# Attention feeding a weighted expert layer on one core: another order of evacuations, sums and first products

## The chip, the cores and the metric

The kernel runs on one core of one Trainium2 chip. The metric is the device time of one launch in microseconds (us). A profile is one execution, recorded by the hardware profiler. Engines are written as in the profile: PE is the matrix engine (PEld its weight loads), DVE the vector engine, ACT the scalar engine, POOL the GpSimd engine, SP the engine that only issues transfers. Each engine works through its own list of instructions in order; semaphores hold one back until another engine or a transfer has delivered.

## The reference, cut to what matters

First a block-sorted attention, for 4 batches of 8 heads with 768 tokens of 64 numbers. A learned 8x8 matrix per head is normalised five times over rows and columns (Sinkhorn); it then mixes the 8 blocks of keys and of values, and each block of 96 queries attends to its own mixed block. After that, four experts with two layers each, weighted per token:

```
P = sort_net;  5 times: P = exp(P - max); P /= row sums; P /= column sums
k_sorted = P @ blocks of k;  v_sorted = P @ blocks of v
attn = softmax(q_block @ k_sorted_block^T / 8) @ v_sorted_block     # 96 x 96 per block
x = attn as (3072 tokens, 512)
p = domain_probs / its row sum
out = sum over e of p[:, e] * (relu(x @ w1[e]) @ w2[e])             # 512 -> 1024 -> 512
```

## The kernel before, in words

The 3072 tokens are 12 chunks of 256: chunk (b, c) is the c-th third of batch b, and g = 3b + c. The program is a single list of calls; the order of the calls is the order of instructions on each engine. While the expert layer works on batch b, the attention of batch b + 1 is done in small stages between its products. `PLANS[b]` says in which slot each stage is issued: an entry (c, n, stage, batch, pair) means slot n of chunk (b, c). In the first layer of a chunk (`chunk_first`, L770) slot 2e + g' follows half g' of expert e: 16 matmuls (L780), the evacuation with ReLU and token weight on DVE (L786), and, for some halves, sums of hidden blocks on DVE (`h_sums`, L744). The stages that matter here, all for a pair of heads:

- `st_k`, `st_v` (L388, L357): block mixing of keys and values on PE. ACT copies the result out; `st_v` for an odd pair then issues six transfers on the SP queue that lay the values out as `vs` (L375).
- `st_s` (L409): scores, into two PSUM tiles; ACT takes the exponentials (L421).
- `st_a` (L438): attention times values, again two PSUM tiles; DVE takes reciprocals and products (L430, L431) out of each tile. It needs `vs`.
- `st_x` (L457), `st_q` (L380): transposing transfers on SP; `st_n`, `st_lk`, `st_lv`: loads issued from POOL.

All stage tiles come from one PSUM pool, `psA`, with two buffers: a stage that asks for a tile waits until the reader of the tile before the last has finished. The first-layer tiles have a pool of their own, `psM`, with two buffers as well.

From batch 1's last chunk on (g = 5, called lead; then the pairs of chunks g = 6/7, 8/9, 10/11) both layers of an expert use a seven-product form (Strassen's scheme) on quarter blocks. In the first layer one unit of work `seven(g, n)` has the products p1 to p7, which use two alternating banks X and two banks Z, and four banks Q:

- p1: Z = a11 b11, and ACT copies Z into X (L1124). p2: Z += a12 b21, and `finish` on DVE (L1110) evacuates Z into the hidden block (0,0).
- p6: X += n2 n2, ACT copies X to u2 (L1131). p7: X += s3 t3, ACT copies X to u3 (L1139), DVE adds t22 = Q + u3 (L1140).
- p4: X += a22 t4, and `finish` on DVE evacuates X into block (1,0).
- p5: Q = s1 t1. p3: Q += s4 b22, DVE adds t12 = Q + u2 (L1148).
- `22` and `12`: ReLU on ACT (L1116) of t22 and t12, then the weighting on POOL (L1117) into blocks (1,1) and (0,1).

The loop in `last_first` overlaps unit e (`now`) with the rest of unit e - 1 (`prev`): now p1, prev p7, the `12` of unit e - 2, now p5, now p2, now p6, prev `22`, prev p4, prev p3. A pair of chunks has eight units of 28 matmuls with 256 columns; lead has units 1 to 3 in this loop, with 56 matmuls of 128 columns each.

The second layer (`chunk` for g = 1 and 2 from L866, `last_second` for g from 5 on) consists of products over all experts (`times`, L764, or `product`, L1217), which need the sums of hidden blocks from DVE: `h_sums` 1 (L750) and 2 (L752), then 3 (L754) and 4 (L756). Its products run in the order b11, b21, n4, t1 (needs sums 1), t2 (sums 2), b22 for the first `early` experts (sums 4), t3 (sums 3), b22 for the other experts. For g = 1 and 2 the order is b11, b21, part of n4, t1, t2, the rest of n4, t3, b22, and the product t2 is added to the output on DVE (L884) before t3 reuses its PSUM bank.

Of the kernel before, what the change touches and what calls it, by code (L numbers as in the profile page):

```python
# [12 lines left out]
ALU = mybir.AluOpType  # L13
# [4 lines left out]
def kernel(  # L18
# [18 lines left out]
    E = moe_w1.shape[0]  # L37
# [571 lines left out]
    def st_bk(b, qd):  # L609
# [16 lines left out]
            (2, 9, st_k, 2, 0), (2, 9, st_lv, 3, 0), (2, 9, st_n, 3, 0), (2, 11, st_s, 2, 0), (2, 12, st_q, 2, 2),  # L626
        ],
        1: [
            (0, 0, st_k, 2, 1), (0, 0, st_bk, 2, 1), (0, 1, st_lk, 3, 0), (0, 1, st_n, 3, 1), (0, 2, st_a, 2, 0), (0, 2, st_q, 2, 3),
            (0, 3, st_v, 2, 2), (0, 3, st_n, 3, 2), (0, 4, st_s, 2, 1), (0, 4, st_x, 2, 0), (0, 5, st_k, 2, 2),  # L630
            (0, 5, st_n, 3, 3), (0, 6, st_v, 2, 3), (0, 6, st_lv, 3, 1), (0, 7, st_s, 2, 2), (0, 8, st_k, 2, 3),
            (0, 8, st_bv, 3, 0), (0, 9, st_bk, 3, 0), (0, 9, st_lk, 3, 1), (0, 9, st_q, 3, 0), (0, 10, st_a, 2, 1),
            (0, 11, st_s, 2, 3), (0, 12, st_a, 2, 2), (0, 12, st_x, 2, 1), (0, 12, st_q, 3, 1), (0, 13, st_v, 3, 0),
# [110 lines left out]
    def h_sums(e, which, own=False, hb=None):  # L744
        h = Hb[:, homes.get(e, e)] if hb is None else hb(e)
        blk = lambda kh, tok: h[:, ds(kh * KH, KH), ds(tok * P, P)]
        sm = [Sb[:, n, e].rearrange("p (f x) -> p f x", f=KH) for n in range(4)]
        tt = nc.vector.tensor_tensor
        if which == 1:
            tt(sm[0], blk(0, 1), blk(1, 1), ALU.add)  # L750
        elif which == 2:
            tt(sm[1], sm[0], blk(0, 0), ALU.subtract)  # L752
        elif which == 3:
            tt(blk(0, 1) if own else sm[2], blk(0, 0), blk(0, 1), ALU.subtract)  # L754
        else:
            tt(blk(1, 0) if own else sm[3], blk(1, 0), sm[1], ALU.subtract)  # L756

    def times(ps, lhs, rhs, es, first=True, done=True, between=None, at=None):

        for e in es:  # L760
            if e == at:
                between()
            for f in range(KH):
                nc.tensor.matmul(  # L764
                    ps, lhs(e, f), Ts[e][rhs][:, f, :],
                    start=(first and e == es[0] and f == 0), stop=(done and e == es[-1] and f == KH - 1),
                    skip_group_check=True,
                )
# [28 lines left out]
    def chunk(b, c, slot, done=()):  # L797
# [68 lines left out]
        if c:  # L866
            both = ob.rearrange("p (h d) -> p h d", h=2)
            times(bankA, blk(0, 0), "b11", es)
            slot()
            times(bankB, blk(1, 0), "b21", es)  # L870
            slot()
            tt(oa1, bankA, oa1, ALU.add)
            tt(oa1, bankB, oa1, ALU.add)
            h_sums(E - 1, 2)
            times(bankC, blk(1, 1), "n4", es[:1], True, False)
            times(bankQ, sm(0), "t1", es)
            tt(ob2, bankQ, ob2, ALU.add)
            slot()
            for e in es:
                h_sums(e, 3)  # L880
            for e in es:
                h_sums(e, 4)
            times(bankA, sm(1), "t2", es, False)
            tt(oa2, bankA, oa2, ALU.add)  # L884
            slot()
            next(sums0)
            times(bankC, blk(1, 1), "n4", es[1:], False)
            tt(ob1, bankC, ob1, ALU.add)
            slot()
            times(bankA, sm(2), "t3", es, False)  # L890
            tt(both, bankA.rearrange("p (o d) -> p o d", o=1).broadcast_to([P, 2, DH]), both, ALU.add)
            slot()
            store(1, ob)
            next(sums0)
            times(bankQ, sm(3), "b22", es, False)
            tt(oa2, bankQ, oa2, ALU.add)
            slot()
            store(0, oa)
            return
# [180 lines left out]
    def seven(g, n):  # L1080

        lead = g == G0
        if lead:
            e, f0, cols = n, 0, P
            pb = pbs[divmod(g, R // 2)]
            home = lambda i, j: Hb[:, e, ds(i * KH, KH), ds(j * P, P)]
            weight = lambda j: pb[:, ds(e, 1), ds(j * P, P)]
            n -= 1
            Q = last["Q"][(0, 0, 1, 3)[e]][:]
        else:  # L1090
            e, f0, cols = n // 2, n % 2 * 2, 2 * P
            home = lambda i, j: (last["H"][e] if j else Hb[:, e])[:, ds(i * KH + f0, 2), :]
            weight = lambda j: pbs[g](j, e)
            Q = last["Q"][n % 4][:]
        m = 512 // cols
        a, t = As[e], Bs[g]
        X, Z = [last[nm][n % len(last[nm])][:] for nm in ("X", "Z")]
        u2, u3, t22, t12 = [last[nm][n % len(last[nm])] for nm in ("u2", "u3", "t22", "t12")]
        tt = nc.vector.tensor_tensor

        def product(dst, lhs, rhs, first=False):
            for f in range(m):
                for k in range(2):
                    nc.tensor.matmul(  # L1104
                        dst[:, ds(f * cols, cols)], a[lhs][:, k, ds((f0 + f) * P, P)], t[rhs][:, k, :],
                        start=(first and f == 0 and k == 0), stop=(f == m - 1 and k == 1), skip_group_check=True,
                    )

        def finish(i, j, src):
            nc.vector.scalar_tensor_tensor(  # L1110
                out=home(i, j), in0=src.rearrange("p (f x) -> p f x", f=m), scalar=0.0,
                op0=ALU.max, in1=weight(j).broadcast_to([P, m, cols]), op1=ALU.mult,
            )

        def finish2(i, j, src):
            nc.scalar.activation(src, src, AF.Relu, bias=0.0, scale=1.0)  # L1116
            nc.gpsimd.tensor_tensor(  # L1117
                home(i, j), src.rearrange("p (f x) -> p f x", f=m),
                weight(j).broadcast_to([P, m, cols]), ALU.mult,
            )  # L1120

        def p1():
            product(Z, "a11", "b11", True)
            nc.scalar.copy(X, Z)  # L1124

        def p5():
            product(Q, "s1", "t1", True)

        def p6():
            product(X, "n2", "n2")  # L1130
            nc.scalar.copy(u2, X)  # L1131

        def p2():
            product(Z, "a12", "b21")
            finish(0, 0, Z)

        def p7():
            product(X, "s3", "t3")
            nc.scalar.copy(u3, X)  # L1139
            tt(t22, Q, u3, ALU.add)  # L1140

        def p4():
            product(X, "a22", "t4")
            finish(1, 0, X)

        def p3():
            product(Q, "s4", "b22")
            tt(t12, Q, u2, ALU.add)  # L1148

        return {  # L1150
            1: p1, 2: p2, 3: p3, 4: p4, 5: p5, 6: p6, 7: p7,
            22: lambda: finish2(1, 1, t22), 12: lambda: finish2(0, 1, t12),
        }

# [5 lines left out]
    def last_first(g, slot=None):  # L1160
        b, c = divmod(g, R // 2)
        lead = int(g == G0)
        if lead:
            chunk_first(b, c, [0], 0, slot)
            last_banks(0)
            last_tmp(g)
            prs = {1: seven(g, 1)}
            prs[1][1]()
            prs[1][5]()
            seven(g, 2)[5]()  # L1170
            prs[1][6]()
            prs[1][2]()
            input_sums(0, 0, True)
            input_sums(0, 1, True)
            last_banks(1)
        else:
            last["e0"][2]()
            prs = {0: last["e0"]}
        N7 = E if lead else 2 * E
        for e in range(1 + lead, N7):  # L1180
            prs[e] = seven(g, e)
        for e in range(1 + lead, N7):
            now, prev = prs[e], prs[e - 1]
            now[1]()
            prev[7]()
            if e > 1 + lead:
                prs[e - 2][12]()
            if not lead or e > 2:
                now[5]()
            now[2]()  # L1190
            now[6]()
            prev[22]()
            prev[4]()
            prev[3]()
        now[7]()
        prev[12]()
        return now

    def last_second(g, now=None, upper=False):
# [12 lines left out]
        def product(ps, lhs, rhs, first=True, es=range(E), between=None, at=E - 1, part=ds(0, DH)):  # L1212
            for e in es:
                if e == at and between:
                    between()
                for f in range(KH):
                    nc.tensor.matmul(  # L1217
                        ps, lhs(e, f), Ts[e][rhs][:, f, part],
                        start=(first and e == 0 and f == 0), stop=(e == E - 1 and f == KH - 1), skip_group_check=True,
                    )  # L1220
# [27 lines left out]
            sums(e, 2)  # L1248
        product(bankC, blk(1, 1), "n4")
        nc.scalar.copy(ob1, bankC)  # L1250
        for e in range(E):
            sums(e, 4, True)
        if lead:
            for e in range(E):
# [8 lines left out]
        if not lead:  # L1263
            for e in range(E):
                sums(e, 3, True)
        early = 1 if final else 2
        for bank, part, _ in ends:
            product(bank[:, part], blk(1, 0), "b22", False, range(early), part=part)
        if closing and not final:
# [201 lines left out]
```

The softmax here doesn't subtract the row's maximum and nothing guards it: scores larger than these inputs give would overflow.

## Time and profile before

| | before |
|---|---|
| median of 4 runs | 364.1 us (362.56 to 364.68) |
| the profiled execution, its own time | 364.41 us |
| span in its profile | 362.6 us |
| PE busy | 352.7 us, 97% of the span |
| DVE busy | 272.0 us, 75% |
| ACT busy | 172.4 us, 48% |
| POOL busy | 133.5 us, 37% |
| granted PE clock | 0.9 of full speed or more in all 40 slices |

The span runs from the first to the last profiled instruction; the 1.8 us between it and the execution's own time lie around it. Start times below are counted from the span's start. In a timeline, a row gives the start and the duration of an instruction or of a group of like ones (x16), the engine, the line and the tiles (out<-in); brackets at its end give the idle time of its engine before it and what ended that. Matmuls overlap, so the time between the starts of two groups tells more than their durations.

### The profile page before, as it was taken

Reading aid. Unit: us, or ns where it says so; the run is one execution under the profiler, and the core shown is the slowest. Engines: PE = TensorE matmul, PEld = TensorE weight load, DVE = VectorE, ACT = ScalarE, POOL = GpSimd, SP = SyncE. Lnnn points to the kernel's source line nnn. Section 1 sums busy time; section 2 is a strip of 40 time slices with the busy share of each in tenths; the row PEclk is TensorE's granted clock in tenths of the full one; section 3 lists DMA queues with packets and bytes.
Section 4 is the critical chain, followed back from the end, with each engine's and each line's share of the span. In section 5 each row is a group of like instructions: output and inputs, shape, how many; then the busy total and the mean of one; then the engine's idle time right before and its main releaser. Section 6 shows DMA issues by size and latency. Waiting matters only on the chain.

```text
span 362.6 us, 9496 instructions
## 1 busy us (share of the span) xinstructions
PE 352.7 (97%) x3949; PEld 305.3 (84%) x3949; DVE 272.0 (75%) x549; ACT 172.4 (48%) x306; POOL 133.5 (37%) x148
## 2 busy tenths in 40 slices
PE   8799999999999899999999999999999999999995
PEld 8685858888888788888889888888888888888895
DVE  5654897779698677868878977895587876677962
ACT  2664330453325255367937258830388611688210
POOL 8882010476022240000526318840068800288300
PEclk9999999999999999999999999999999999999999
DMA  8999999999999999935996310005200014100011
GB/s 110 207 207 230 214 209 198 193 181 191 196 165 132 188 137 160 158 94 73 166 206 77 108 69 0 2 2 117 107 12 2 3 57 118 61 0 2 2 72 46
DMA packets 72007, 40.52 MB, mean 112 GB/s; under 512 B 40598, under 2 KB 66716, under 8 KB 71964
## 3 DMA queue, kind: packets, MB, share of 16 engines
q0 software_dynamic: 36560, 19.93, 42.0%
q1 hardware_dynamic: 35260, 19.92, 29.2%
q8 instruction: 31, 0.51, 0.6%
q14 instruction: 12, 0.10, 0.1%
q10 hardware_dynamic: 144, 0.07, 0.1%
HBM read 42.13 MB, written 6.34 MB: 134 GB/s over the span
## 4 chain that ended last, share of the span: by engine, by line
PE 84%; DMA 7%; DVE 5%; ACT 1%; SPq 1%; POOL 1%; issue 1%; ACTq 0%; DVEq 0%
PE ps_Q L1217 17%; PE ps_h L780 16%; PE ps_X L1104 10%; PE ps_p L764 8%; PE ps_Z L1104 7%; PE ps_Q L1104 7%; PE ps_Z L1217 6%; DMA w<-in_moe_w_dram 4%; PE ps_o L704 3%; PE ps_p L815 3%; DMA vs<-arena 2%; PE ps_h L669 1%; PE ps_a L449 1%; PE ps_s L414 1%; PE ps_v L361 1%; SPq L375 1%
## 5 line engine op out<-in xcount | busy, mean ns | idle before, releaser
L780 PE MATMUL ps_h<-xT,w 128*128 128x256 f16 x576 | 67.7, 273 | 0.0
L780 PEld LDWEIGHTS <-w 128*128 128x128 f16 x576 | 55.2, 98 | 7.3
L786 DVE SCALAR_TENSOR_TENSOR Hb<-ps_h,pb 128x1024 f16<-128x1024 f32 x34 | 41.5, 1224 | 17.3 <-PE ps_h L780 17.1
L1104 PEld LDWEIGHTS <-w 128*128 128x128 f16 x480 | 43.5, 98 | 6.4 <-issue 0.3
L1117 POOL TENSOR_TENSOR arena<-tmp,pb 128x512 f16<-128x512 f32 x12 | 15.3, 1275 | 65.8 <-PE ps_Z L1104 49.9
L1217 PEld LDWEIGHTS <-Hb 128*128 128x128 f16 x320 | 31.2, 98 | 3.6
L1116 ACT ACTIVATE tmp<-tmp 128x512 f32<-128x512 f32 x46 | 29.3, 638 | 3.2 <-DVE tmp L1148 2.6
L1217 PEld LDWEIGHTS <-Sb 128*128 128x128 f16 x304 | 28.2, 98 | 3.0
L1104 PEld LDWEIGHTS <-arena 128*128 128x128 f16 x312 | 27.7, 98 | 2.9
L421 ACT ACTIVATE ET<-ps_s 96x768 f16<-96x768 f32 x24 | 18.0, 802 | 25.4 <-PE ps_s L414 25.2
L404 ACT CAST kT<-ps_k 64x384 f16<-64x384 f32 x48 | 22.7, 473 | 14.1 <-PE ps_k L395 13.1
L121 POOL DMA_DIRECT2D arena<-in_q_dram x24 | 19.9, 842 | 19.5 <-DMA q_ring<-arena 19.1
L1104 PE MATMUL ps_X<-ET,arena 128*128 128x256 f16 x168 | 25.2, 272 | 0.0
L1124 ACT COPY ps_X<-ps_Z 128x512 f32<-128x512 f32 x27 | 15.4, 570 | 19.9 <-PE ps_Z L1104 15.6
L764 PEld LDWEIGHTS <-Hb 128*128 128x128 f16 x232 | 21.9, 98 | 3.0
L1217 PE MATMUL ps_Q<-w,Hb 128*128 128x256 f16 x192 | 24.4, 273 | 0.0
L1104 PE MATMUL ps_Z<-xT,w 128*128 128x256 f16 (+1 forms) x176 | 22.5, 257 | 0.2 <-ACT ps_X L1124 0.2
L1140 DVE TENSOR_TENSOR tmp<-ps_Q,tmp 128x512 f32<-128x512 f32 x20 | 13.8, 691 | 11.3 <-ACT tmp L1139 7.6
L1110 DVE SCALAR_TENSOR_TENSOR Hb<-ps_X,pb 128x512 f16<-128x512 f32 x27 | 18.4, 682 | 1.6 <-PE ps_X L1104 1.6
L750 DVE TENSOR_TENSOR Sb<-Hb 128x512 f16<-128x512 f16 x33 | 19.5, 610 | 0.0
L1131 ACT COPY tmp<-ps_X 128x512 f32<-128x512 f32 x26 | 15.2, 586 | 9.1 <-PE ps_X L1104 8.8
L1110 DVE SCALAR_TENSOR_TENSOR Hb<-ps_Z,pb 128x512 f16<-128x512 f32 x27 | 18.4, 682 | 1.3 <-PE ps_Z L1104 1.3
(261 smaller groups left out, 743.5 us busy)
## 6 DMA issues: line engine op xcount, KB each, us to landing
w<-in_moe_w_dram POOLq DMA_DIRECT2D x7, 1024.0 KB, 28.3
pb<-p_dram SPq DMA_DIRECT2D x9, 512.0 KB, 7.1
arena<-in_k_dram POOLq DMA_DIRECT2D x8, 384.0 KB, 10.2
arena<-in_v_dram POOLq DMA_DIRECT2D x8, 384.0 KB, 8.5
vs<-arena SPq DMA_DIRECT2D x36, 66.0 KB, 6.0
arena<-in_q_dram POOLq DMA_DIRECT2D x24, 96.0 KB, 9.7
out_dram<-ob SPq DMA_DIRECT2D x9, 256.0 KB, 2.1
out_dram<-oa SPq DMA_DIRECT2D x8, 256.0 KB, 2.3
```

The source lines that it names most:

```text
L121: nc.gpsimd.dma_start(t[:, h // 2, :, h % 2, :], q[b, h].rearrange("(t p) d -> p t d", p=P))
L404: nc.scalar.copy(kT[ds(D * hh, D), r], pk[ds(D * r, D), hh].rearrange("p a (i c) -> p a i c", c=CP),)
L421: nc.scalar.activation(ETs[2 * (pr % 2) + hh][:, 0:S].rearrange("c (a x) -> c a x", a=2), pss[hh][0:BLK, :, 0:HS], AF.Exp, bias=0.0, scale ...
L750: tt(sm[0], blk(0, 1), blk(1, 1), ALU.add)
L764: nc.tensor.matmul(ps, lhs(e, f), Ts[e][rhs][:, f, :], start=(first and e == es[0] and f == 0), stop=(done and e == es[-1] and f == KH - 1 ...
L780: nc.tensor.matmul(ps[:, f, :], w1sb[e][:, kc, ds((4 * g + f) * P, P)], xT[:, kc, ds(2 * c * P, 2 * P)], start=(kc == 0), stop=(kc == NKC ...
L786: nc.vector.scalar_tensor_tensor(out=Hb[:, homes.get(e, e), ds(4 * g, 4), :], in0=ps[:], scalar=0.0, op0=ALU.max, in1=weights(e).broadcast ...
L1104: nc.tensor.matmul(dst[:, ds(f * cols, cols)], a[lhs][:, k, ds((f0 + f) * P, P)], t[rhs][:, k, :], start=(first and f == 0 and k == 0), st ...
L1110: nc.vector.scalar_tensor_tensor(out=home(i, j), in0=src.rearrange("p (f x) -> p f x", f=m), scalar=0.0, op0=ALU.max, in1=weight(j).broadc ...
L1116: nc.scalar.activation(src, src, AF.Relu, bias=0.0, scale=1.0)
L1124: nc.scalar.copy(X, Z)
L1217: nc.tensor.matmul(ps, lhs(e, f), Ts[e][rhs][:, f, part], start=(first and e == 0 and f == 0), stop=(e == E - 1 and f == KH - 1), skip_gro ...
```

## The change

It moves instructions and adds none to PE, ACT, POOL or SP; the work done is the same.

1. **Plan of batch 1.** `st_a(2,0)` goes from slot 2 to slot 3 of chunk (1,0), its `st_x` from slot 4 to 5, and `st_v(2,2)` from slot 3 to slot 5, behind `st_k(2,2)`.
2. **Chunks g = 1 and 2.** The sums 4 are issued behind the product t2 and its addition (L884), not ahead of them.
3. **Pairs.** The `finish` of Z moves behind p4 of the unit before, so that DVE evacuates X ahead of Z. PE's order stays.
4. **Lead.** In the loop for e = 2 the p5 of unit 3 is placed ahead of p2, and p3 of unit 1 moves from the end of that round into the round for e = 3, where p5 was; `12` of unit 1 follows it.
5. **`last_second`.** Outside lead, the sums 4 of experts 2 and 3 move behind the sums 3. In the last chunk `early` is 2, not 1.

```diff
         1: [
-            (0, 0, st_k, 2, 1), (0, 0, st_bk, 2, 1), (0, 1, st_lk, 3, 0), (0, 1, st_n, 3, 1), (0, 2, st_a, 2, 0), (0, 2, st_q, 2, 3),
-            (0, 3, st_v, 2, 2), (0, 3, st_n, 3, 2), (0, 4, st_s, 2, 1), (0, 4, st_x, 2, 0), (0, 5, st_k, 2, 2),
+            (0, 0, st_k, 2, 1), (0, 0, st_bk, 2, 1), (0, 1, st_lk, 3, 0), (0, 1, st_n, 3, 1), (0, 2, st_q, 2, 3), (0, 3, st_a, 2, 0),
+            (0, 3, st_n, 3, 2), (0, 4, st_s, 2, 1), (0, 5, st_x, 2, 0), (0, 5, st_k, 2, 2), (0, 5, st_v, 2, 2),
             (0, 5, st_n, 3, 3), (0, 6, st_v, 2, 3), (0, 6, st_lv, 3, 1), (0, 7, st_s, 2, 2), (0, 8, st_k, 2, 3),
...
             for e in es:
                 h_sums(e, 3)
+            times(bankA, sm(1), "t2", es, False)
+            tt(oa2, bankA, oa2, ALU.add)
             for e in es:
                 h_sums(e, 4)
-            times(bankA, sm(1), "t2", es, False)
-            tt(oa2, bankA, oa2, ALU.add)
             slot()
...
+        def p2_first():
+            product(Z, "a12", "b21")
+
+        def p2_last():
+            finish(0, 0, Z)
+
...
-            1: p1, 2: p2, 3: p3, 4: p4, 5: p5, 6: p6, 7: p7,
+            1: p1, 2: p2, 3: p3, 20: p2_first, 21: p2_last, 4: p4, 5: p5, 6: p6, 7: p7,
...
             now[1]()
             prev[7]()
-            if e > 1 + lead:
+            if lead:
+                (prs[3][5] if e == 2 else prs[1][3])()
+                now[2]()
+                now[6]()
+                prev[22]()
+                prev[4]()
+                if e > 2:
+                    prs[1][12]()
+                    prev[3]()
+                continue
+            if e > 1:
                 prs[e - 2][12]()
-            if not lead or e > 2:
-                now[5]()
-            now[2]()
+            now[5]()
+            now[20]()
             now[6]()
             prev[22]()
             prev[4]()
+            now[21]()
             prev[3]()
...
         nc.scalar.copy(ob1, bankC)
-        for e in range(E):
+        early = 2
+        for e in range(E if lead else early):
             sums(e, 4, True)
...
             for e in range(E):
                 sums(e, 3, True)
-        early = 1 if final else 2
+            for e in range(early, E):
+                sums(e, 4, True)
```

## The prediction

> **What bounds the kernel now.** I read the shares of busy time first, then PE's own waits, then the chain of work that ended last, and from it the timeline of each place that the change touches.
>
> ```profile
> PE 352.7 (97%) x3949; PEld 305.3 (84%) x3949; DVE 272.0 (75%) x549; ACT 172.4 (48%) x306; POOL 133.5 (37%) x148
> ```
>
> PE is busy in 97% of the span, and the chain gives it 84%. No edit removes a matmul, so a gain can only be a gap on PE that closes, and a loss one that opens. In steady work sixteen matmuls of 256 columns take 1.75 us from start to start (chain: "PE ps_h L780 x16"), so one is 0.109 us and four are 0.44 us; I take each gap from start times against this. Four places matter.
>
> Place one, chunk (1,0):
>
> ```profile
> 119.47 3.66 PE L780 MATMUL ps_h<-xT,w 128*128 128x256 f16 x32
> 124.83 0.65 PE L449 MATMUL ps_a<-vs,ET 96*128 96x65 f16 x16 [1.70 <-DMA vs<-arena]
> 125.27 0.20 DVE L430 RECIPROCAL rz<-ps_a 96x8 f32<-96x8 f32 x1 [0.88 <-PE ps_a L449]
> 126.35 0.69 DVE L431 TENSOR_TENSOR xsl<-ps_a,rz 96x512 f16<-96x512 f32 x1
> 127.26 1.23 DVE L786 SCALAR_TENSOR_TENSOR Hb<-ps_h,pb 128x1024 f16<-128x1024 f32 x1 [0.23 <-PE ps_h L780]
> 128.85 0.42 DVE L752 TENSOR_TENSOR Sb<-Sb,Hb 128x512 f16<-128x512 f16 x1
> 129.23 0.51 PE L414 MATMUL ps_s<-q_ring,kT 64*128 64x96 f16 x16
> ```
>
> 32 matmuls from 119.47 are over at 119.47 + 3.49 = 122.96; `st_a(2,0)` starts at 124.83, when its `vs` has landed. That is a gap of 1.87 us, the largest after the opening. While PE stands, DVE is free to empty `st_a`'s tiles at once, from 125.27 to 126.35 + 0.69 = 127.04.
>
> Place two, chunk g = 1 (and the same row in g = 2):
>
> ```profile
> 88.98 1.04 PE L764 MATMUL ps_p<-T,Hb 128*128 128x256 f16 x8
> 90.34 1.47 PE L764 MATMUL ps_p<-T,Sb 128*128 128x256 f16 x12 [0.32 <-DVE room L884]
> ```
>
> Eight matmuls from 88.98 end at 89.85; t3 starts at 90.34, 0.49 late, since L884 stood in DVE's queue behind the sums 4. In g = 2 the same pair of rows (113.16 and 114.21) gives 0.18.
>
> Place three, a round of a pair:
>
> ```profile
> 226.54 0.60 PE L1104 MATMUL ps_X<-ET,w 128*128 128x256 f16 x4
> 226.83 0.68 DVE L1110 SCALAR_TENSOR_TENSOR Hb<-ps_Z,pb 128x512 f16<-128x512 f32 x1
> 227.43 0.68 DVE L1110 SCALAR_TENSOR_TENSOR Hb<-ps_X,pb 128x512 f16<-128x512 f32 x1
> 228.03 0.68 DVE L1148 TENSOR_TENSOR tmp<-ps_Q,tmp 128x512 f32<-128x512 f32 x1
> 228.22 0.57 ACT L1124 COPY ps_X<-ps_Z 128x512 f32<-128x512 f32 x1 [0.29 <-DVE Hb L1110]
> 228.28 0.60 PE L1104 MATMUL ps_Q<-kT,arena 128*128 128x256 f16 x4
> 228.84 0.60 PE L1104 MATMUL ps_Z<-xT,w 128*128 128x256 f16 x4
> 229.40 0.69 DVE L1140 TENSOR_TENSOR room<-ps_Q,room 128x512 f32<-128x512 f32 x1 [0.69 <-ACT room L1139]
> ```
>
> p5 starts at 228.28, p2 at 228.84: 0.56 where 0.44 is due. p2 waits for the copy L1124, that waits for DVE to empty X, and DVE empties Z first.
>
> Place four, lead's second layer:
>
> ```profile
> 200.50 2.57 DVE L750 TENSOR_TENSOR Sb<-Hb 128x512 f16<-128x512 f16 x3
> 201.33 1.46 POOL L1117 TENSOR_TENSOR Hb<-tmp7x,pb 128x512 f16<-128x512 f32 x1 [0.28 <-ACT tmp7x L1116]
> 203.19 1.91 PE L1217 MATMUL ps_Q<-w,Sb 128*128 128x256 f16 x16
> 203.33 0.41 DVE L750 TENSOR_TENSOR Sb<-Hb 128x512 f16<-128x512 f16 x1
> ```
>
> The sums that PE uses from 203.19 are ready hardly before; the last one waits for POOL's last multiplication, which ends at 202.79.
>
> **The change, part by part.** *Plan.* One slot later, `st_a` stands behind the sixteen matmuls of (1, second half), which now start at 122.96 and end at 124.71; `vs` allows 124.83, so 0.12 of the 1.87 stays. But DVE's queue has changed too: the evacuation of that half and two sums now stand ahead of `st_a`'s four instructions. Today this block runs 1.95 us behind its matmuls and takes 128.85 + 0.42 - 127.26 = 2.01; so 122.96 + 1.95 + 2.01 = 126.92, and `st_a`'s tiles are empty 1.77 later (127.04 - 125.27), at 128.69. `st_s(2,1)` asks for both tiles: `st_v(2,2)`, which lay between and took one, is gone. PE is ready at 124.83 + 0.48 + 1.84 = 127.15 and starts some 0.1 after DVE, about 128.8: a wait of 1.65. Queued behind it is everything on PE. `st_v(2,2)` comes 0.33 us of PE work later, behind `st_k(2,2)`; `st_v(2,3)` then needs the tile of `st_k`, which ACT copies for 1.96 us (one L404 group, now from 131.6 to 133.5), about 0.2 more than PE gives it. The SP queue gets the next six `vs` issues 0.3 later; their reader starts 3.8 us after they land today (142.3 and 146.1), which hides it. `st_x` and the loads have no near reader. Sum: -1.87 + 0.12 + 1.65 + 0.2 = **+0.1 us**. The wait changes its name from DMA to DVE.
>
> *Chunks g = 1, 2.* L884 follows t2 at once and is over before t3 is due (88.95 + 0.42 against 89.85). The sums 4 end about 0.5 us later; their reader, b22, starts at 91.6, they end at 90.4. **-0.49 - 0.18 = -0.7 us.**
>
> *Pairs.* X is emptied first: p4 starts at 226.54, and DVE follows a p4 by 0.64 where it is free (198.37 to 199.01), so X starts at 227.18, not 227.43; L1124 can then follow Z's first product. The chain's p2 rows in this pair are 0.48, 0.48, 0.56, 0.55, 0.56 for 0.44 due: 0.43 in all, and the other two pairs read alike. The other side: Z starts at 227.78 and L1148 at 228.38, 0.35 later. L1148 is over at 229.06, before L1140 can start (229.40, less the 0.17 that the copies gain on ACT: L1124 starts 0.81 after p1 today, 0.64 then). **3 x -0.43 = -1.3 us.**
>
> *Lead.* p5 of unit 3 fills the gap ahead of p2 of unit 2 (0.38: 191.62 where 191.24 was due). Yet the next p2 waits for L1124, that for DVE's X, which goes by DVE's queue (input sums until 192.29, then three evacuations), unchanged. With as much PE work ahead of it, that p2 starts at 194.82 as today: the gap moves. What does change is POOL: `12` of unit 1, at 195.88 today, goes behind `22` of unit 2, whose ReLU ends about 197.0. Five multiplications of 1.3 follow without a pause and end near 203.8, not 202.79. The fourth L750 then ends about 1.1 late. Today it ends at 203.74 and PE needs it at 203.19 + 1.31 = 204.50: 0.76 of cover, so PE waits **+0.3 us**. The bounds are 0 (DVE keeps its pace) and 1.1 (all of it reaches PE).
>
> Three L750 took 2.57 us here, against 0.415 for the median one: something beside POOL slows them. The Trainium skill, "SBUF — State Buffer", section "Who interferes with whom", says that a DVE instruction with two SBUF inputs and a GpSimd instruction that reads SBUF exclude one another for a whole instruction. That speaks against this edit, which puts one more multiplication beside these sums; taken strictly, a further sum loses a whole multiplication, and the term would be the upper bound, 1.1, not 0.3.
>
> *`last_second`.* Its sums come in the order of use now; no gap stands there today (96 matmuls in 10.48 us is 0.109 each). In the last chunk t3 waits 0.23 for ACT's copy L1262 (eight b22 matmuls of half width from 354.88 end at 355.32, t3 starts 355.55). Eight more fill that, but then DVE's three last additions follow t3 without a pause and bind: **-0.1 us.**
>
> Sum: +0.1 - 0.7 - 1.3 + 0.3 - 0.1 = -1.7 us. The profiled execution took 364.41, so 362.7; it lies 0.3 above the median of 364.1, against which the forecast is **362.4 us**.
>
> **The rivals.** *The later `st_a` pays in full.* If DVE empties its tiles before 127.15, the first term is -1.7, the time 360.6. For it: the wait on `vs` is plain in the profile. Against it: the queue above. The same pattern, `st_a` one slot ahead of `st_s`, starts today at 144.04, 0.1 behind DVE's second L431, with nothing queued ahead on DVE.
>
> *The pairs do not gain.* p2 may be held by the copy itself: L1124 follows p1 by 0.64 and takes 0.57, p2 needs it 1.31 after p1's start, so the cover is 0.1. If that is lost, the pair term is 0, the time 363.7.
>
> *Slower: L1140 slides in the pairs.* DVE now stands until p4 is through and does Z and L1148 after it. Should L1148 push L1140 by its own 0.35, then p3, due 0.06 after L1140's end (226.97 and 226.91), waits 0.29 in 7 rounds of 3 pairs, 6.1 us: 364.1 + 6.1 - 1.7 = 368.5. It decides at L1140 starting more than 1.87 us after its round's p1, since p3 falls due 6 x 0.44 = 2.62 after p1; today it is 1.99 with the gap in the round (227.41 to 229.40), and 1.81 is what I expect. Against it: 0.15 us between L1148's end and L1140's start.
>
> **How the numbers follow.** What can be told from no change is about 0.5%, 1.8 us: the bounds are 362.3 and 365.9. My forecast (0.55) lies at the edge, 0.29 beyond and 0.26 within. Full pay 0.17 (faster), no gain in the pairs 0.17 (within), sliding 0.11 (slower). Faster 0.46, same 0.43, slower 0.11. The range goes from full pay, a little rounded, 360.4, to the case where the pairs gain nothing and lead costs its upper bound, 363.7 + 0.8 = 364.5.
>
> **What would show it.** Right: `st_a` without a wait for DMA, `st_s(2,1)` idle 1.6 us for DVE L431; no wait for the bank's addition before t3; p2 rows of 0.44 in the pairs' chain, and L1124 released by PE; in lead one gap of 0.5 before unit 3's p2 and L1217 waiting for L750. Wrong: `st_s` starting before 128 us, p2 rows still at 0.55, or waits of p3 for L1140.

## The result, and the profile after

| | before | after |
|---|---|---|
| median | 364.6 us (78 runs) | 362.92 us (54 runs) |
| ratio to before, 95% interval | | 0.996 (0.9951 to 0.997) |
| the profiled execution, its own time | 364.41 us | 363.6 us |
| span in its profile | 362.6 us | 361.7 us |

The change makes the kernel 1.5 us faster (0.4%; the interval is 1.1 to 1.8 us). The forecast was 1.7 us, a time of 362.4 in a range of 360.4 to 364.5. The gain lies just inside the 0.5% that the prediction drew as its border; it gave this side 0.43 and a larger gain 0.46. The ratio leaves out the executions more than 1.5% above the fastest (3 of 54 and 4 of 78).

The page after, engine by engine: busy time, share of the span, instructions.

```profile
PE 352.2 (97%) x3949; PEld 305.9 (85%) x3949; DVE 275.2 (76%) x549; ACT 172.4 (48%) x306; POOL 133.2 (37%) x148
```

The counts are those of before. PE is 0.5 us less busy, and DVE 3 us busier with the same instructions, among them L750, whose durations sum to 26.8 us and before to 25.1 (0.9 of the difference lies in place four). The edits shift line numbers: L1148 is now L1154, L1217 is L1233, L1262 is L1279, and L884 is L882.

The view of waits, for PE, names what PE now stands for (in total, times, longest); these are its largest rows beside those of the opening (L312, L256, L563):

```profile
PE ps_s L414 <- DVE xsl L431: 1.3, 2, 0.7
PE ps_h L780 <- DMA xT<-xsl: 0.4, 1, 0.4
PE ps_a L449 <- DMA vs<-arena: 0.3, 1, 0.3
```

The 1.7 us of `st_a(2,0)` for `vs` is gone, and 1.3 us of the scores for DVE stands in its place. L884's (now L882's) wait is gone. The wait on `vs` that is left is another one, at 182 us. The timeline of place one, chunk (1,0), from `st_a` on (of the timelines here, the rows that matter):

```profile
125.08 0.65 PE L449 MATMUL ps_a<-vs,ET 96*128 96x65 f16 x16
125.28 1.22 DVE L786 SCALAR_TENSOR_TENSOR Hb<-ps_h,pb 128x1024 f16<-128x1024 f32 x1 [0.52 <-PE ps_h L780]
125.56 1.91 PE L780 MATMUL ps_h<-xT,w 128*128 128x256 f16 x16
...
126.87 0.42 DVE L752 TENSOR_TENSOR Sb<-Sb,Hb 128x512 f16<-128x512 f16 x1
127.21 0.20 DVE L430 RECIPROCAL rz<-ps_a 96x8 f32<-96x8 f32 x1
128.19 0.21 PE L414 MATMUL ps_s<-q_ring,kT 64*128 64x96 f16 x1 [0.71 <-DVE xsl L431]
128.28 0.69 DVE L431 TENSOR_TENSOR xsl<-ps_a,rz 96x512 f16<-96x512 f32 x1
129.02 0.51 PE L414 MATMUL ps_s<-q_ring,kT 64*128 64x96 f16 x15 [0.62 <-DVE xsl L431]
```

`st_a` starts without a wait. DVE has L786, L750 (126.42) and L752 to do before L430 can begin at 127.21, and the second L431 ends at 128.97. The sixteen matmuls from 125.56 are over at 127.31. The first score matmul starts when the first tile is empty, and the other fifteen, which need the second, at 129.02. One matmul of the scores takes some 0.03, so the loss is 129.02 - 127.31 - 0.03 = 1.68 us.

Place two, t3's start in chunk g = 1, and place three, a round of a pair, in the timeline after:

```profile
89.50 1.04 PE L764 MATMUL ps_p<-T,Hb 128*128 128x256 f16 x8
90.37 1.47 PE L764 MATMUL ps_p<-T,Sb 128*128 128x256 f16 x12
```

```profile
227.69 0.69 DVE L1110 SCALAR_TENSOR_TENSOR Hb<-ps_X,pb 128x512 f16<-128x512 f32 x1 [0.27 <-PE ps_X L1104]
227.92 0.60 PE L1104 MATMUL ps_Z<-xT,w 128*128 128x256 f16 x4
...
228.29 0.68 DVE L1110 SCALAR_TENSOR_TENSOR Hb<-ps_Z,pb 128x512 f16<-128x512 f32 x1
228.60 0.57 ACT L1124 COPY ps_X<-ps_Z 128x512 f32<-128x512 f32 x1 [0.16 <-PE ps_Z L1104]
228.79 0.60 PE L1104 MATMUL ps_Q<-kT,arena 128*128 128x256 f16 x4
...
229.23 0.60 PE L1104 MATMUL ps_Z<-xT,w 128*128 128x256 f16 x4
229.78 0.69 DVE L1140 TENSOR_TENSOR room<-ps_Q,room 128x512 f32<-128x512 f32 x1 [0.21 <-ACT room L1139]
```

t3 follows after 0.87, the eight matmuls' own time. In the pair p2 follows p5 by 0.44 (228.79 to 229.23), where it took 0.56. The copy L1124 is released by PE (p1, from 227.92) and no longer by DVE. L1140 is held by ACT's copy, not by L1154. Place four, the second layer of lead:

```profile
195.31 0.61 PE L1104 MATMUL ps_Z<-xT,w 128*128 128x128 f16 x8 [0.29 <-ACT ps_X L1124]
200.99 3.49 DVE L750 TENSOR_TENSOR Sb<-Hb 128x512 f16<-128x512 f16 x3
201.33 2.87 POOL L1117 TENSOR_TENSOR Hb<-tmp7x,pb 128x512 f16<-128x512 f32 x2
203.67 2.14 PE L1233 MATMUL ps_Q<-w,Sb 128*128 128x256 f16 x16
204.74 0.41 DVE L750 TENSOR_TENSOR Sb<-Hb 128x512 f16<-128x512 f16 x1
```

The gap before unit 2's p2 is gone, and one of 0.46 stands before unit 3's (195.31, where 194.85 was due). POOL has two multiplications left beside the three sums, not one; the sums take 3.49 us and not 2.57, and the fourth starts 1.07 after the product that uses it, not 0.14. That product takes 1.98 from start to the next one's start where 1.75 is due.

Matched matmul by matmul, the span's 0.89 us (after less before) divides as follows:

| stretch | us |
|---|---|
| opening: first weights arrive later (PE's L704 at 28.48, before 27.96) | +0.52 |
| chunks g = 1 and 2, L884's waits | -0.48, -0.18 |
| a wait for transposed x at 118.09 | +0.52 |
| plan, chunk (1,0) from `st_a` to 134 us | -0.06 |
| around 182 us: a wait on `vs` +0.46, one on DVE gone -0.28 | +0.18 |
| lead | +0.23 |
| three pairs | -1.33 |
| last chunk | -0.28 |

The parts that were changed sum to -2.1. The other +1.2 (opening, 118 us, 182 us) lies in stretches that the change doesn't touch. That the wait at 118 us comes from PE being earlier there, after part 2, isn't borne out: the profile of part 2 alone has no such wait. A second profile of the changed kernel (the last experiment) has neither of the two later waits, and a span of 361.0.

### The profile page after: what moved, and what is told of

It reads as the page before. It is cut to its first block, busy times and chain, and to the rows that moved or that the text cites. A ratio compares the mean times of both kernels' runs of the same rounds, so it can differ in the third digit from the quotient of the medians.

```text
span 361.7 us, 9496 instructions
## 1 busy us (share of the span) xinstructions
PE 352.2 (97%) x3949; PEld 305.9 (85%) x3949; DVE 275.2 (76%) x549; ACT 172.4 (48%) x306; POOL 133.2 (37%) x148
## 4 chain that ended last, share of the span: by engine, by line
PE 85%; DVE 7%; DMA 3%; issue 2%; ACT 2%; DVEq 0%; ACTq 0%
PE ps_Q L1233 16%; PE ps_h L780 16%; PE ps_p L764 9%; PE ps_X L1104 9%; PE ps_Q L1104 6%; PE ps_Z L1104 6%; PE ps_Z L1233 6%; PE ps_h L669 3%; PE ps_o L704 3%; PE ps_p L815 3%; DMA xT<-xsl 2%; PE ps_s L414 1%; PE ps_a L449 1%; DVE xsl L431 1%; DVE Sb L750 1%
## 5 line engine op out<-in xcount | busy, mean ns | idle before, releaser
L786 DVE SCALAR_TENSOR_TENSOR Hb<-ps_h,pb 128x1024 f16<-128x1024 f32 x34 | 41.5, 1223 | 18.7 <-PE ps_h L780 18.4
L1233 PEld LDWEIGHTS <-Hb 128*128 128x128 f16 x320 | 31.1, 98 | 3.6
L1233 PEld LDWEIGHTS <-Sb 128*128 128x128 f16 x304 | 28.0, 98 | 3.4 <-DVE Sb L750 0.3
L404 ACT CAST kT<-ps_k 64x384 f16<-64x384 f32 x48 | 22.7, 473 | 14.5 <-PE ps_k L395 13.5
L1233 PE MATMUL ps_Q<-w,Hb 128*128 128x256 f16 x192 | 24.4, 273 | 0.0
L1124 ACT COPY ps_X<-ps_Z 128x512 f32<-128x512 f32 x27 | 15.4, 570 | 18.5 <-PE ps_Z L1104 18.2
L750 DVE TENSOR_TENSOR Sb<-Hb 128x512 f16<-128x512 f16 x33 | 21.2, 660 | 0.0
L1154 DVE TENSOR_TENSOR tmp<-ps_Q,tmp 128x512 f32<-128x512 f32 x26 | 17.7, 682 | 0.8 <-PE ps_Q L1104 0.8
```

Source lines behind the costliest of these rows:

```text
L404: nc.scalar.copy(kT[ds(D * hh, D), r], pk[ds(D * r, D), hh].rearrange("p a (i c) -> p a i c", c=CP),)
L786: nc.vector.scalar_tensor_tensor(out=Hb[:, homes.get(e, e), ds(4 * g, 4), :], in0=ps[:], scalar=0.0, op0=ALU.max, in1=weights(e).broadcast ...
L1233: nc.tensor.matmul(ps, lhs(e, f), Ts[e][rhs][:, f, part], start=(first and e == 0 and f == 0), stop=(e == E - 1 and f == KH - 1), skip_gro ...
```

## The experiments

Theory: the gain is that of parts 2 and 3, with a little from 5; parts 1 and 4 move a wait and are worth about nothing. Rival: part 1 or 4 carries a part of the gain. All ratios are against the kernel before, run on the same chip beside them, with 95% intervals; 0.001 is 0.36 us. The edits are shortened.

**Part 1 alone** (plan).

```diff
-(0, 2, st_a, 2, 0) ... (0, 3, st_v, 2, 2) ... (0, 4, st_x, 2, 0)
+(0, 3, st_a, 2, 0) ... (0, 5, st_x, 2, 0) ... (0, 5, st_v, 2, 2)
```

> Only the plan's three entries are changed, everything else is the kernel before. Theory (the wait moves from DMA to DVE): ps_a starts without a wait for DMA, the next scores wait for DVE L431 for 1.3 to 1.7 us, ps_v(2,3) starts 0.2 late; sum within 0.2 us of the kernel before. Rival (the later stage pays in full): no wait of the scores, 1.7 us faster.

Measured: 1.0007 (0.999 to 1.0023), +0.25 us. The profile has the wait of the scores and none for `vs`:

```profile
124.69 0.65 PE L449 MATMUL ps_a<-vs,ET 96*128 96x65 f16 x16
127.79 0.21 PE L414 MATMUL ps_s<-q_ring,kT 64*128 64x96 f16 x1 [0.71 <-DVE xsl L431]
128.63 0.51 PE L414 MATMUL ps_s<-q_ring,kT 64*128 64x96 f16 x15 [0.62 <-DVE xsl L431]
```

The rival that the later `st_a` pays in full falls: the wait changes its name, and the time does not change measurably.

**Part 2 alone** (sums 4 behind t2).

```diff
-            for e in es: h_sums(e, 4)
             times(bankA, sm(1), "t2", es, False)
             tt(oa2, bankA, oa2, ALU.add)
+            for e in es: h_sums(e, 4)
```

> Only the order of the sums 4 and the product t2 in the chunks g = 1 and 2 is changed. Theory: t3 starts on time in both chunks, 0.49 and 0.18 us gained there; what is gained in g = 2 may be lost at once, since the first matmuls of the next chunk then wait for the transposed x (the changed kernel's profile shows 0.52 us there), so 0.3 to 0.7 us faster. Rival (the later sums 4 make b22 late): no gain.

Measured: 0.9982 (0.9965 to 0.9999), -0.65 us. L884's wait is gone in both chunks.

**Part 3 alone** (X evacuated ahead of Z in the pairs).

```diff
-            now[2]()
+            now[20]()        # p2's product alone
...
             prev[4]()
+            now[21]()        # the finish of Z
```

> Only the order of the evacuations of Z and X in the three pairs is changed. Theory: the p2 rows fall from 0.48 to 0.56 us to 0.44, 0.43 us per pair, 1.3 us faster in all; this is most of the gain of the whole change. Rival (copy L1124 itself holds p2, or L1140 slides): p2 rows unchanged or p3 rows longer, no gain or a loss.

Measured: 0.9954 (0.9935 to 0.9974), -1.7 us. Its p2 rows follow p5 by 0.44, as in the whole change. Both rivals about the pairs (no gain; L1140 sliding) fall.

**Part 4 alone** (lead's order).

```diff
             if lead:
+                (prs[3][5] if e == 2 else prs[1][3])()
                 now[2]()
...
+                if e > 2:
+                    prs[1][12]()
+                    prev[3]()
+                continue
```

> Only lead's round is re-ordered. Theory: the gap before p2 of unit 2 (0.38 us) goes and one of about 0.46 us opens before p2 of unit 3; POOL's multiplications end about 1 us later beside the sums L750, of which three take some 3.5 us instead of 2.57, and the product t1 takes 0.2 to 0.3 us more; 0.2 to 0.3 us slower than the kernel before. Rival (the filled gap is a gain): 0.4 us faster.

Measured: 1.0013 (0.9997 to 1.0029), +0.5 us. The gap stands before unit 3's p2 with the same 0.46, and the second layer is 0.23 longer.

**All parts but lead's.** The change without the edit just shown.

> The changed kernel with lead's round as before. Theory: a little faster than the changed kernel, by 0.2 to 0.5 us, so 1.7 to 2.1 us faster than the kernel before; the three L750 of lead take 2.57 us again. Rival (the filled gap helped): 0.4 us slower than the changed kernel.

Measured: 0.9941 (0.9917 to 0.9966), -2.1 us, against -1.5 for the whole. Lead's old gap (0.38 before unit 2's p2) is back and its second layer has its old length. The two intervals overlap, but together with part 4 alone they put part 4 on the side of a loss, though neither comparison is clear of zero by itself.

**Part 5 alone** (last chunk and order of the sums).

```diff
-        early = 1 if final else 2
+        early = 2            # and sums 4 of experts 2, 3 behind the sums 3
```

> Only the second layer's order of sums and the last chunk's early b22 are changed. Theory: nothing but the last chunk moves, t3 there starts without its 0.23 us wait for L1262, 0.1 to 0.2 us faster than the kernel before, not to be told from no change. Rival (the later sums 4 of two experts hold the last b22): PE rows of b22 late, up to 0.5 us slower per chunk.

Measured: 0.9987 (0.9964 to 1.001), -0.5 us, an interval that holds zero. t3 no longer waits for the copy of t2's result.

**The scores later.** If the scores' wait for DVE is the price of part 1, more PE work ahead of the scores should take it back.

```diff
-(0, 4, st_s, 2, 1), (0, 5, st_x, 2, 0), (0, 5, st_k, 2, 2), (0, 5, st_v, 2, 2), (0, 5, st_n, 3, 3),
-(0, 6, st_v, 2, 3), (0, 6, st_lv, 3, 1), (0, 7, st_s, 2, 2), (0, 8, st_k, 2, 3), (0, 8, st_bv, 3, 0),
+(0, 5, st_x, 2, 0), (0, 5, st_s, 2, 1), (0, 5, st_n, 3, 3), (0, 6, st_v, 2, 2), (0, 6, st_k, 2, 2),
+(0, 7, st_v, 2, 3), (0, 7, st_lv, 3, 1), (0, 8, st_s, 2, 2), (0, 8, st_bv, 3, 0), (0, 9, st_k, 2, 3),
```

> The changed kernel with the scores of pair (2,1) a slot later still, so that DVE has emptied both tiles of ps_a before PE asks for them; value and key stages follow one slot later each, values first. Theory (the plan's gain was lost to the tiles that DVE empties late): the scores start without a wait, ps_v(2,3) too, 1.6 to 1.8 us faster than the changed kernel, 3.1 to 3.4 us faster than before. Rival (something else is late next, a copy on ACT or the landing of the next values): the gap turns up again within the next slots and the time stays within 0.5 us of the changed kernel.

Measured: 0.9955 (0.9937 to 0.9972), -1.6 us: no gain over the change. Its PE rows:

```profile
129.31 0.52 PE L414 MATMUL ps_s<-q_ring,kT 64*128 64x96 f16 x16
130.31 1.91 PE L780 MATMUL ps_h<-xT,w 128*128 128x256 f16 x16 [0.48 <-DVE Hb L786]
142.34 1.91 PE L764 MATMUL ps_p<-T,Sb 128*128 128x256 f16 x16 [0.51 <-DVE oa L842]
```

The scores start at once. The next half of the first layer then waits for its own PSUM tile, since DVE does `st_a`'s four instructions before that evacuation, and later an addition is late behind ACT's copies. From `st_a` at 125.23 to the first product of the next chunk at 151.18 this kernel takes 25.95 us, the change from 125.08 to 151.35 takes 26.27: the scores' 1.68 and the 0.2 of `st_v(2,3)` are gone, and all but 0.3 of them comes back, a part behind DVE's queue and a part behind ACT's. That is the rival.

**Lead's input sums later.** The gap before unit 3's p2 was put down to DVE's queue, which has two input sums (L978) ahead of the evacuations.

```diff
-            input_sums(0, 0, True)
-            input_sums(0, 1, True)
             last_banks(1)
...
             now[1]()
+            if lead and e == 3:
+                input_sums(0, 0, True)
+                input_sums(0, 1, True)
             prev[7]()
```

> The changed kernel with lead's two input sums on DVE (L978, 1.28 us) moved behind unit 3's p1, where DVE stands 1.2 us. Theory (DVE's queue with those sums ahead holds X and with it p2 of unit 3): the gap of 0.46 us before that p2 goes, POOL's chain ends about as late as in the changed kernel; 0.3 to 0.5 us faster than the changed kernel. Rival (p2 is held by PE's own order or by ACT): the gap stays, no gain.

Measured: 0.9971 (0.9954 to 0.9989), -1.1 us: not faster than the change. The gap shrinks only to 0.35: with the sums gone DVE stands 1.01 us for ACT's copy L1139 before unit 1's L1140 (191.28), and X is empty at 193.17 all the same. The two sums (on DVE from 193.09) now take 2.36 us, beside a multiplication on POOL, where they took 1.28; they delay L1140, for which p3 waits:

```profile
193.21 1.68 POOL L1117 TENSOR_TENSOR Hb<-tmp,pb 128x512 f16<-128x512 f32 x1 [2.88 <-ACT tmp L1116]
195.37 0.68 DVE L1140 TENSOR_TENSOR tmp<-ps_Q,tmp 128x512 f32<-128x512 f32 x1
196.10 0.61 PE L1104 MATMUL ps_Q<-xT,w 128*128 128x128 f16 x8 [0.70 <-DVE tmp L1140]
```

The second of the two takes 1.76, from 193.69 to 195.45, for 0.68 in the change. L1140's other input, ACT's copy, was ready at 194.36. This place was wrong for them, and the run does not tell what a better one would bring.

**Parts 2, 3 and 5**, with plan and lead as before.

> Parts 2, 3 and 5 alone; plan and lead as before. Theory (the gain lies in the sums of chunks 1 and 2, in the pairs and in the last chunk, while plan and lead together are worth nothing or a small loss): -0.65 - 1.7 - 0.5 by the three kernels that have one of these parts each, -2.3 by the profile's steps (0.7, 1.3 and 0.1 to 0.3); so 2.0 to 2.8 us below before, a ratio of 0.992 to 0.9945, and 0.5 to 1.3 us below the whole change. Rival (plan and lead carry part of the gain): no lower than the whole change, a ratio of 0.996 or more.

Measured: 0.9955 (0.9936 to 0.9974), -1.6 us. The theory asked for a ratio of 0.992 to 0.9945 and its rival for 0.996 or more: the measured one lies between and decides for neither. The run shows that the gain is there without parts 1 and 4; whether those two cost anything together can't be told from these runs.

**Extra PE work ahead of `st_a`**, in the kernel before and in part 1 alone.

```diff
+                again = (b, c, e, g) == (1, 0, 0, 0)
-                for f in range(4):
+                for f in ((0, 1) if again else ()) + (0, 1, 2, 3):
```

> The kernel before, with the first eight matmuls of chunk (1,0)'s first half done twice, 0.87 us of PE work that changes no result, between the issue of vs and st_a's wait for it. Theory (vs lands at a time of its own, so the wait for it takes up what makes PE late): the wait for vs is shorter by 0.87 or gone, and the time grows by the part that the wait does not cover. With the waits seen so far before st_a (1.87, 0.97, 0.84, 0.39, 0.08) the mean cover is 0.61, so 0.26 us slower than before. Rival (the time of vs follows PE): 0.87 us slower, and the wait in the profile as long as in the kernel before.

> Part 1 alone with the same 0.87 us of extra PE work. Theory (here the scores wait for DVE, which follows PE by a fixed chain, so nothing takes up a late PE): 0.87 us slower than part 1 alone, which read +0.25, so some 1.1 us above before and 0.6 above the kernel before with the same extra work; the scores' wait for DVE stays at 1.3 us. Rival (the new wait has slack as well): within 0.3 us of the kernel before with the extra work, and the scores' wait shorter.

Measured: 1.0011 (0.9996 to 1.0027), +0.4 us, in the kernel before; 1.0036 (1.0018 to 1.0054), +1.3 us, with part 1, which is 1.06 more than part 1 alone. The two kernels' PE rows, first before's, then part 1's:

```profile
125.76 0.65 PE L449 MATMUL ps_a<-vs,ET 96*128 96x65 f16 x16 [0.94 <-DMA vs<-arena]
```

```profile
129.00 0.21 PE L414 MATMUL ps_s<-q_ring,kT 64*128 64x96 f16 x1 [0.71 <-DVE xsl L431]
129.84 0.51 PE L414 MATMUL ps_s<-q_ring,kT 64*128 64x96 f16 x15 [0.62 <-DVE xsl L431]
```

With part 1 the wait keeps its 0.71 and 0.62, and from `st_a` to the scores' second start it is 3.94 us without the extra work (124.69 to 128.63) and 3.95 with it (125.89 to 129.84): the extra 0.87 is paid in full, and the chain from PE through DVE back to PE has no slack. How much the transfer covers in the kernel before, this run doesn't tell: the interval of the +0.4 (-0.15 to +1.0) holds the theory's 0.26 and its rival's 0.87, and the wait in the profile is 1.10 by start times. The expectation worked with waits from one execution each; start times show how far these differ. From the matmul of `st_v(2,1)`, whose copy feeds `vs`, to `st_a` (one execution of each kernel with the plan of before):

| kernel | `st_v(2,1)` | PE ready | `st_a` | wait | `st_v` to `st_a` |
|---|---|---|---|---|---|
| before | 111.35 | 122.96 | 124.83 | 1.87 | 13.48 |
| part 2 alone | 111.24 | 122.67 | 123.64 | 0.97 | 12.40 |
| part 3 alone | 112.12 | 123.72 | 123.72 | 0 | 11.60 or less |
| part 4 alone | 112.29 | 124.17 | 125.00 | 0.83 | 12.71 |
| part 5 alone | 111.18 | 122.78 | 123.18 | 0.40 | 12.00 |
| parts 2, 3, 5 | 111.70 | 123.13 | 124.04 | 0.91 | 12.34 |
| before, extra work | 112.18 | 124.66 | 125.76 | 1.10 | 13.58 |

PE's own way from `st_v` to `st_a` is 11.4 to 11.9 us without the extra work. The way of the values through ACT, six issues and the transfers differs by execution. All fourteen traces have the landing of the last of the six, whether PE waited for it or not: 11.4 to 13.5 us after that matmul. The wait is the difference. For the twelve executions without extra work, and PE's own way taken as 11.6, that makes (an estimate) a wait of 0 to 1.9 in the order of before, 1.0 in the mean, and the profile of before holds the longest.

**Lead without two multiplications.** It was to show whether POOL slows the sums.

```diff
+            if g == G0 and n == 3:
+                ...              # ReLU by ACT straight into the block
+                return
```

> The whole change, but the weighting of unit 3's blocks (1,1) and (0,1) in lead is left out (ACT's ReLU writes these blocks itself), so that the last two multiplications of POOL are gone and none runs beside lead's sums. Theory (the sums are slow because of POOL's multiplications beside them): the three L750 take 0.42 each, 1.3 us or less where they start behind POOL's last one and 1.7 at most with one multiplication beside the first, not 3.49; the product t1 waits for none of them, lead's second layer is 0.23 shorter or more, and the time 0.2 to 0.5 us below the whole change. Rival (they wait for their data or for PE): three L750 still over 2.5 us.

In lead the function lowers `n` by one, so the condition never held: nothing was left out, and this is the whole change a second time. Measured: 0.9971 (0.9949 to 0.9993), which agrees with 0.996. Its three L750 take 3.50 us beside POOL's two multiplications, where the first profile has 3.49.

That POOL is the cause was not tested by taking it away. What the traces show beside that stands in the last section.

## Why the prediction was right, step by step

*Plan, +0.1.* The mechanism held: the scores lose 1.68 us for DVE where 1.65 was forecast, the second start is 129.02 where some 128.8 was forecast (`st_a` itself came 0.25 later than assumed), and `st_v(2,3)` is 0.2 late as worked out. Against this one execution the step measures -0.06, in runs +0.25 (-0.4 to +0.8). What was weak is the first term, -1.87: it came from the execution with the longest wait, and the mean by the landings above is 1.0. With that and the 1.68 and 0.2 that the scores and `st_v(2,3)` lose, plan would cost about +0.9, which the runs don't show either: part 1 alone ends its interval at +0.8, and parts 2, 3 and 5 measure -2.1 with part 1 (all parts but lead's) and -1.6 without. So that +0.1 came out near the runs is in part luck, and what takes up the rest is open.

*Chunks 1 and 2, -0.7.* In the profile -0.48 and -0.18, in runs -0.65.

*Pairs, -1.3.* In the profile -1.33, in runs -1.7 (-2.4 to -0.95). The slower rival was nearer than its 0.11 says. It decides at L1140 starting more than 1.87 after its round's p1. The change has 227.92 to 229.78, 1.86, where 1.81 was expected. What holds it is the copy L1139 on ACT, straight behind L1124, which PE releases, and not L1154; so the queue on DVE has 0.21 of room, but p3 none. The other rival was near as well: L1124 ends at 228.60 + 0.57 = 229.17, 0.06 before p2, where the cover was put at 0.1.

*Lead, +0.3.* The profile has +0.23; runs of part 4 alone +0.5 (-0.1 to +1.05). The gap moved as forecast (0.46 for "about 0.5"), POOL ends 1.4 later, and the fourth L750 starts 0.93 later against its product, of which 0.76 was covered. One reading was not right: the fourth L750 doesn't wait for POOL's last multiplication itself (over at 202.79 before, 204.20 after) but stands in DVE's queue behind the third, slowed sum (over at 203.07 and 204.48) and one addition to the output. The Trainium skill's rule ("SBUF — State Buffer", section "Who interferes with whom") fits the sums: one more of them takes 1.49 and not 0.41, which is 1.08, close to a whole multiplication. But the upper bound of 1.1 drawn from it left out the cover of the product, and the trace's row decides: +0.23.

*Last chunk, -0.1.* The mechanism is as forecast: DVE's last additions start at 357.17, 357.51, 357.84 and 358.04 without a pause, where the last stood 0.31 for PE before. The size was off, -0.28 in the profile: DVE's last one ends at 358.32 for 359.13, 0.8 sooner, of which 0.61 was PE's lead from earlier; the last 0.1 lies behind it, in the store. Alone, part 5 measures -0.5 (-1.3 to +0.4), too wide to tell.

The sum of the steps was -1.7, the profile's -2.1 and the sum of the parts alone +0.25 - 0.65 - 1.7 + 0.5 - 0.5 = -2.1. The whole change measures -1.5 (1.1 to 1.8). Each part's interval is 0.6 to 0.8 us to either side, so the difference of 0.6 is within them.

## What to carry to other kernels

When a consumer is put later to hide a transfer, ask who empties its result: here a wait of PE for a DMA became a wait of PE for DVE of nearly the same length, and putting the next consumer later as well only handed it on, to waits behind DVE and ACT. The sure gains were reorderings on a queue that PE already waited for (DVE's sums and evacuations in order of use), at no cost that a row shows. A wait for a transfer read off one execution is one draw; look at several before crediting its full length.

## What the hardware showed that was not expected

The time from `st_v` to the landing of `vs` differs by up to 2 us between executions of nearly the same program, and the first expert weights reach PE between 27.79 and 29.12 us after the span's start. A profile of the same program can thus differ by 0.7 us in its span (361.7 and 361.0 for the change) without any edit.

In the trace of the change 169 of the 180 sums on DVE (L750 to L756) have no computing POOL instruction beside them, and none of these takes over 0.43 us, POOL's issues of transfers beside some of them notwithstanding. Of the eleven that have one, five take 1.48 to 1.49: two in lead and one in the second layer of each pair (from 239, 288 and 337 us), where PE doesn't wait for them. The multiplications of POOL beside those five take 1.44 to 1.46, all others of this shape 1.26 to 1.29.

Two things in the traces speak for POOL as the cause. In all fourteen, 130 of these sums take over 0.5 us, and every one of them ends 0.28 to 0.29 us after a computing POOL instruction that ran beside it has ended. One that was already running when POOL's began keeps its 0.41 (in the profile of before, from 201.25, with POOL's from 201.33). And the slow sums move with the multiplications: in the nine kernels with lead as before, the third L750 of lead takes 1.48 to 1.49 and the second 0.41, in the five with part 4 both take 1.48 to 1.49. A wait for data is not it: the third sum belongs to expert 2, whose last multiplication is over at 201.38 in the change, and it starts at 203.00. No run here took POOL's work away.
